# Query maxima of the first six head pairs: from a product with minus the identity to rows laid out through DRAM

## The chip, the cores and the metric

One NeuronCore of a Trainium2 chip runs the whole program. The metric is the device time of one execution in microseconds (us); a version's time is the median of its runs. The core has a matrix engine (PE, with its weight loads shown as PEld), a vector engine (DVE), an activation engine (ACT), a general engine (POOL) and a queue engine (SP) from which every DMA of this kernel is issued. Each engine takes its instructions strictly in the order in which the program holds them.

## The reference

Eight batches of eight heads of 576 tokens go through an attention with exponential features; its output goes through a two-layer network with a squared ReLU.

```python
# q, k, v: (8, 8, 576, 64); w_phi: (64, 128); w_in: (512, 2048); w_out: (2048, 512); all float32
def phi(x):
    proj = einsum('bhsd,df->bhsf', x, w_phi)
    proj = proj - max(abs(proj), axis=-1, keepdims=True)
    return concatenate([exp(proj), exp(-proj)], axis=-1)
q_p, k_p = phi(q), phi(k)
kv  = einsum('bhsf,bhsd->bhfd', k_p, v);  z = sum(k_p, axis=2)
num = einsum('bhsf,bhfd->bhsd', q_p, kv)
den = einsum('bhsf,bhf->bhs', q_p, z)[..., None] + 1e-06
x = (num / den) as (4608 tokens, 512)
out = square(maximum(x @ w_in, 0)) @ w_out
```

What matters here is the subtraction in `phi` for the queries: from all 128 features of a token the largest absolute feature of that token is taken away before the two exponentials.

## The kernel before, in words

**Tiling.** Two heads make a pair, and there are 32 pairs `p`, four to a batch. The query tile `q` of a pair has the 64 dimensions of head 0 on partitions 0 to 63, those of head 1 on partitions 64 to 127, and the 576 tokens along the row. The key tile `k` is alike. The network runs over 18 chunks `c` of 256 tokens, each in 8 steps `f` of 256 hidden columns: `gemm1` (24 fp16 products of 128x256, since inputs and weights are split into a high and a low half) and `gemm2` (12 products of 128x512). A chunk can start when the pairs that hold its tokens have put their output into `ring`; chunk 0 needs pairs 0 to 3. The weights come in as raw 1 MB blocks (`raw0i` to `raw7i`, `raw0o` to `raw7o`) and are split by ACT, DVE and POOL (`prep`).

**Early and late pairs.** Pairs 0 to 5 are the early ones (`EARLY = 6`, function `early`), pairs 6 to 31 the late ones (`visit` and `late`). A late pair finds its query maxima on POOL. An early pair goes through these steps:

- `k_main`, `k_tail`, `keys`: features of the keys, with tokens on partitions, their maxima, differences and exponentials `e` and `et`;
- `kv_main`, `ends`, `flip`: the products of key features with `v` and with ones, and a turn of their sum into `kz`;
- `q_main` and `q_tail`: features of the queries with tokens on partitions, wanted only for the maxima. Three reductions on DVE put them into `qm`: columns 0 to 3 for head 0, 4 to 7 for head 1, 128 tokens to a column, and column 8 for the last 64 tokens of both heads;
- `q_proj`, twice (`c` = 0 and 1, 288 tokens each): the features again, now with features on partitions, in the PSUM tile `pp`. To this product the kernel adds a second one that takes the maxima away: a column of `qm`, broadcast as weights, times `nident`, minus the identity. A column holds 128 tokens, so each half and head takes three of these products (L665);
- `num` and `dens`, with the exponentials `qe` of that tile; the denominators go out of `sx` through DRAM (`den`, `rd`) and come back as rows `rb`; POOL multiplies, and ACT and DVE write `ring`.

**Order.** The code does not fix the order. Every step is an `Op` with an engine, a planned duration, what it comes after, the buffers that it uses and a rank. `Plan.order` lays the steps out on the five engines by these numbers, and `Plan.improve` moves ranks at random 400 times and keeps what shortens its plan. The program is then written in the order of planned starts, so another set of steps or durations gives another order on every engine, for DMAs on SP too. Tiles have few buffers: `pp` is one, `q` and `k` two, `qe` three. In `Plan.add` for a DMA, `land` is the planned time to its landing.

Of the kernel before, what the change touches and what calls it, by code (L numbers as in the profile page):

```python
# [14 lines left out]
F32 = mybir.dt.float32  # L15
# [11 lines left out]
B, H, S, D = 8, 8, 576, 64  # L27
# [12 lines left out]
SH = S // 2  # L40
# [20 lines left out]
WHOLE, ROWS, COLS, STRIPS = range(4)  # L61
# [196 lines left out]
def dve_us(n):  # L258
    return (n + 151) / 960
# [15 lines left out]
def tile_kernel(ctx, tc, qp, kp, vp, w_phi, w_in, w_out, out):  # L275
    nc = tc.nc
    V, A, G, PE, SP = nc.vector, nc.scalar, nc.gpsimd, nc.tensor, nc.sync
    P = Plan()

    cp = ctx.enter_context(tc.tile_pool(name="const", bufs=1))  # L280
    at = ctx.enter_context(tc.tile_pool(name="attn", bufs=1))
    mp = ctx.enter_context(tc.tile_pool(name="moe", bufs=1))
    sm = ctx.enter_context(tc.tile_pool(name="small", bufs=1))
    dr = ctx.enter_context(tc.tile_pool(name="scratch", bufs=1, space=DRAM))
    ps = ctx.enter_context(tc.tile_pool(name="psum", bufs=1, space=PSUM))

    def sub(eng, out_, a, b_):
        eng.tensor_tensor(out=out_, in0=a, in1=b_, op=ALU.subtract)  # L288

    def tiles(pool, tag, shape, dtype, bufs, first=0):  # L290
        return Tiles(P, pool, tag, shape, dtype, bufs, first)

    ident = cp.tile([128, 128], F32, name="ident")
    ones = cp.tile([128, 32], F32, name="ones")
    nident = cp.tile([128, 128], F32, name="nident")
    mask = cp.tile([128, 2, 32], F32, name="mask")
    wraw = cp.tile([128, 3 * F], F32, name="wraw")
    wbf, wst = wraw[:, 0:2 * F], wraw[:, 2 * F:]
# [15 lines left out]
    kmt_ = tiles(sm, "kmt", [128, 1], F32, 2)  # L314
    kvs_ = tiles(at, "kvs", [128, 384], F32, 1)
    kz_ = tiles(at, "kz", [128, 384], F32, 2)
    pt_ = tiles(at, "pt", [128, 2, S], F32, 1, EARLY)
    mx_ = tiles(at, "mx", [128, S], F32, 1, 2 * EARLY)
    qe_ = tiles(at, "qe", [128, 2 * S], F32, 3)
    n_ = tiles(at, "n", [128, S], F32, 1)  # L320
    yt_ = tiles(at, "yt", [128, S], F32, 1, None)
# [9 lines left out]
    den_ = tiles(sm, "den", [128, 9], F32, 2)  # L331
    rc_ = tiles(sm, "rc", [128, 9], F32, 2)
    rd_ = tiles(dr, "rd", [128, 9], F32, 3)
    td_ = tiles(dr, "td", [128, 256], F32, 2, EARLY)
    rb_ = tiles(at, "rb", [128, S], F32, 2)
    vm_ = tiles(sm, "vm", [128, NP], F32, 2)
    pw_ = tiles(sm, "pw", [128, 2], F32, 2)
    qm_ = tiles(sm, "qm", [128, 9], F32, 2)

    pp_ = tiles(ps, "pp", [128, 2, 512], F32, 1, None)  # L340
    pn_ = tiles(ps, "pn", [128, 512], F32, 1, None)
# [9 lines left out]
    dq = cp.tile([32, 2, 32], F32, name="dq")  # L351
    make_identity(nc, ident)
    V.memset(ones, 1.0)
# [144 lines left out]
    exps, exp_t, sums, kz_of, qexp, dens_of, k_load, q_load, num_in = {}, {}, {}, {}, {}, {}, {}, {}, {}  # L500
# [78 lines left out]
    def early(p):  # L579
# [3 lines left out]
        R = lambda x: base + x  # L583
# [21 lines left out]
        o = P.add("PE", 1.73, lambda: kv_main(p, pv_["s", p]), exps[p] + [v_load[p]], kv[:-1], R(2.0), mode=COLS)  # L605
        o = P.add("PE", 1.66, ends, [o, exp_t[p]], kv, R(2.5), mode=(COLS, STRIPS))
# [7 lines left out]
        o = P.add("PE", 0.35, flip, [o, pool_start], [("kvs", p), ("pv", ("t", p))], R(3.0))  # L614
# [5 lines left out]
        most = []  # L620
# [27 lines left out]
        qe = lambda c: qe_[2 * p + c].rearrange("p (h s x) -> p h s x", h=2, s=2)
        for c in range(2):
            n = 2 * p + c  # L650
            cs = slice(SH * c, SH * c + SH)
            pq = ("pp", ("q", n))

            def q_proj(n=n, cs=cs):
                for h in range(2):
                    PE.matmul(out=pp_["q", n][:, h, 0:SH], lhsT=wst[64 * h:64 * h + 64, :],
                              rhs=q_[p][64 * h:64 * h + 64, cs], start=True, stop=False)
                for h in range(2):
                    for t in range(5):
                        lo, hi = max(cs.start, 128 * t), min(cs.stop, 128 * t + 128)  # L660
                        if lo < hi:

                            i, r, d = (4 * h + t, 0, lo - 128 * t) if t < 4 else (8, 64 * h, 64 * h)
                            rows = slice(r, 128 if t < 4 else r + 64)
                            PE.matmul(out=pp_["q", n][:, h, lo - cs.start:hi - cs.start],  # L665
                                      lhsT=qm_[p][rows, i:i + 1].to_broadcast([rows.stop - r, 128]),
                                      rhs=nident[rows, d:d + hi - lo], start=False, stop=hi == cs.stop)
# [4 lines left out]
            o = P.add("ACT", act_us(576), lambda c=c, src=src: A.activation(
                out=qe(c)[:, :, 1, :], in_=src(), func=AF.Exp, scale=-1.0), [o], [("qe", n), pq], R(x + 0.4))
            qexps.append(P.add("ACT", act_us(576), lambda c=c, src=src: A.activation(
                out=qe(c)[:, :, 0, :], in_=src(), func=AF.Exp), [o], [("qe", n), pq], R(x + 0.4)))
# [27 lines left out]
        use = [("sx", ("d", p))]  # L703
# [126 lines left out]
    def late(p):  # L830
# [21 lines left out]
        def q_proj():  # L852
# [4 lines left out]

        o = P.add("PE", 0.98, q_proj, [q_load[p]], [("q", p)] + pq, R(RQ), mode=ROWS)
        pt = [P.add("ACT", act_us(1024), lambda: A.activation(
            out=pt_[p][:, :, 0:512], in_=pp_["Q", p], func=AF.Copy), [o], [pq[0], ("pt", p)], R(RQ + 0.1))]  # L860
        for h in range(2):
            pt.append(P.add("ACT", act_us(64), lambda h=h: A.activation(  # L862
                out=pt_[p][:, h, 512:S], in_=tail(h), func=AF.Copy), [o], [pq[1 + h], ("pt", p)], R(RQ + 0.1)))
        qexp[p], dens = [], []
        for h in range(2):
            n = 2 * p + h
            qe = lambda s, n=n: qe_[n][:, S * s:S * s + S]
            o = P.add("POOL", par_us(S), lambda n=n, h=h: G.partition_all_reduce(  # L868
                mx_[n], pt_[p][:, h, :], channels=128, reduce_op=bass_isa.ReduceOp.absmax),
                [pt[0], pt[1 + h], pool_next], [("pt", p), ("mx", n)], R(RQ + 0.2), lock=0.0)  # L870
            o = P.add("DVE", dve_us(S), lambda n=n, h=h, qe=qe: sub(V, qe(0), pt_[p][:, h, :], mx_[n]),
                      [o], [("pt", p), ("mx", n), ("qe", n)], R(RQ + 0.3), lock=4.0)
# [13 lines left out]
            o = P.add("DVE", dve_us(S), lambda n=n, y=y: V.transpose(yt_["y", n - 2 * EARLY], y()), [o], [("pt", p), ("yt", ("y", n - 2 * EARLY))], R(RQ + 0.9))  # L886
# [170 lines left out]
```

## Time and profile before

| | |
|---|---|
| median of 3 runs | 1089.73 us (1088.62 to 1090.1) |
| the profiled execution | 1087.31 us, of which the span from first to last instruction is 1085.5 us |
| mean granted TensorE clock | 0.997 |
| PE busy | 1063.7 us (98%) |
| DVE, ACT, POOL busy | 737.3, 632.9, 185.6 us |
| first `gemm1` starts at | 100.62 us |

All durations below are of the one profiled execution, which took 2.42 us less than the median. A group's row gives line, engine, operation, output and input tiles, shapes and count. A row of the timeline gives start, duration, engine, line, operation, and in brackets the idle time ahead of it with what ended it. Neighbouring PE rows overlap, because matmuls are pipelined: the time that a step takes is the distance from its start to the next start.

### The profile page before, as it was taken

The page shows a single profiled execution, that of the slowest core. Times are in us where ns is not written, and L with a number is a line of the kernel's source. Part 1 is how long each engine was busy: PE and PEld are TensorE (multiplying, and loading weights), DVE is VectorE, ACT ScalarE, POOL GpSimd, SP SyncE. Part 2 cuts the span into 40 slices and gives each one's busy share as a digit, 9 for nine tenths or more (in the row PEclk, how much of TensorE's full clock was granted, in tenths as well). Part 3 has the DMA queues.
Part 4 walks back from the last instruction along what each step waited for, and adds up shares of the span by engine and source line. Part 5 has one row for each costly group of instructions (what it writes and reads, how often), then busy time and mean ns, then how long its engine had stood idle before and what let it go on. Part 6 is the DMA issues. An engine that isn't in the chain of part 4 may idle for free.

```text
span 1085.5 us, 19971 instructions
## 1 busy us (share of the span) xinstructions
PE 1063.7 (98%) x7882; PEld 826.3 (76%) x7882; DVE 737.3 (68%) x1537; ACT 632.9 (58%) x1125; POOL 185.6 (17%) x87
## 2 busy tenths in 40 slices
PE   7889999999999999999999999999999999999997
PEld 6656777777777777777777777877777777888886
DVE  4589989787778877877878776776777855112111
ACT  6889864466566665656556655665555645333232
POOL 1366531111111111111111111111100111000000
PEclk9999999999999999999999999999999999999999
DMA  8844412212212122222222111112120101000000
GB/s 304 309 126 117 149 46 68 59 35 56 85 45 85 46 75 55 69 62 57 74 56 75 55 60 38 54 55 75 43 63 22 50 14 41 1 21 20 1 20 20
DMA packets 68288, 73.49 MB, mean 68 GB/s; under 512 B 36836, under 2 KB 41828, under 8 KB 68196
## 3 DMA queue, kind: packets, MB, share of 16 engines
q1 hardware_dynamic: 68196, 72.23, 21.8%
q8 instruction: 62, 1.02, 0.4%
q14 instruction: 30, 0.25, 0.1%
HBM read 59.18 MB, written 12.99 MB: 66 GB/s over the span
## 4 chain that ended last, share of the span: by engine, by line
PE 88%; DVE 4%; ACT 3%; DMA 2%; issue 1%; POOL 1%; SPq 0%; DVEq 0%; POOLq 0%
PE po L962 35%; PE ph L934 33%; PE pv L568 4%; PE pp L512 3%; PE pn L786 3%; PE pp L855 3%; PE pv L786 2%; PE pv L573 1%; PE pp L665 1%; PE pn L518 1%; DVE u L415 1%; DMA k<-in_kp_dram 1%; DMA den<-sx 1%; ACT u L412 1%; POOL u L426 1%
## 5 line engine op out<-in xcount | busy, mean ns | idle before, releaser
L934 PE MATMUL ph<-ring,win 128*128 128x256 f16 x3456 | 399.4, 273 | 0.1
L934 PEld LDWEIGHTS <-win 128*128 128x128 f16 x3456 | 328.2, 98 | 67.9 <-issue 30.2
L962 PE MATMUL po<-wout,gh 128*128 128x512 f32 x1152 | 369.6, 402 | 0.0
L962 PEld LDWEIGHTS po<-wout,gh 128*128 128x128 f32 x1152 | 206.8, 189 | 47.8 <-issue 5.6
L943 ACT ACTIVATE r<-ph,cw 128x512 f32<-128x512 f32 x144 | 98.8, 686 | 234.1 <-PE ph L934 233.9
L962 PE MATMUL po<-wout,gl 128*128 128x512 f32 x576 | 226.3, 393 | 0.0
L868 POOL PARTITION_ALL_REDUCE mx<-pt x52 | 113.6, 2184 | 634.3 <-ACT pt L862 528.3
L288 DVE TENSOR_TENSOR gl<-ph,gh 128x512 fp32r<-128x512 f32 x144 | 98.7, 686 | 166.1 <-ACT ph L952 163.5
L962 PEld LDWEIGHTS po<-wout,gl 128*128 128x128 f32 x576 | 108.1, 188 | 25.1 <-DVE gl L288 0.5
L945 ACT ACTIVATE gh<-r 128x512 fp32r<-128x512 f32 x144 | 90.9, 631 | 4.6
L952 ACT ACTIVATE ph<-r 128x512 f32<-128x512 f32 x128 | 74.7, 583 | 0.0
L808 ACT ACTIVATE n<-pn 128x320 f32<-128x320 f32 x26 | 11.4, 438 | 102.4 <-PE pn L786 102.4
L568 PE MATMUL pv<-e,v 128*64 128x256 f32 x512 | 60.9, 380 | 0.4 <-ACT kz L615 0.4
L882 DVE SCALAR_TENSOR_TENSOR pt<-qe,zc,pt 128x576 f32<-128x576 f32 x52 | 42.2, 813 | 22.4 <-ACT pt L880 21.4
L288 DVE TENSOR_TENSOR qe<-pt,mx 128x576 f32<-128x576 f32 x52 | 39.2, 754 | 22.6 <-POOL mx L868 22.3
L534 ACT ACTIVATE e<-e 128x512 f32<-128x512 f32 x64 | 39.8, 621 | 21.4 <-DVE e L531 21.2
L568 PEld LDWEIGHTS pv<-e,v 128*64 128x64 f32 x512 | 35.5, 137 | 15.1 <-ACT kz L615 0.5
L873 ACT ACTIVATE qe<-qe 128x576 f32<-128x576 f32 x52 | 35.0, 673 | 17.2 <-DVE qe L288 17.1
L819 DVE STREAM_TRANSPOSE kvs<-pv 128x256 f32<-128x256 f32 x26 | 11.6, 445 | 47.7 <-PE pv L786 44.4
L880 ACT ACTIVATE pt<-qe,zc 128x576 f32<-128x576 f32 x52 | 39.6, 771 | 3.3
L886 DVE STREAM_TRANSPOSE yt<-pt 128x576 f32<-128x576 f32 x52 | 40.4, 776 | 1.3
L536 ACT ACTIVATE e<-e 128x512 f32<-128x512 f32 x64 | 40.2, 629 | 1.7
(196 smaller groups left out, 1296.0 us busy)
## 6 DMA issues: line engine op xcount, KB each, us to landing
v<-in_vp_dram SPq DMA_DIRECT2D x32, 320.0 KB
k<-in_kp_dram SPq DMA_DIRECT2D x32, 288.0 KB
q<-in_qp_dram SPq DMA_DIRECT2D x32, 288.0 KB
rb<-rd SPq DMA_DIRECT2D x64, 144.0 KB
out_dram<-o SPq DMA_DIRECT2D x36, 256.0 KB
td<-kvs SPq DMA_DIRECT2D x26, 128.0 KB
kz<-td SPq DMA_DIRECT2D x208, 16.0 KB
raw0i<-in_w_in_dram SPq DMA_DIRECT2D x1, 1024.0 KB
```

Source lines behind the costliest of these rows:

```text
L288: eng.tensor_tensor(out=out_, in0=a, in1=b_, op=ALU.subtract)
L536: exps[p].append(P.add("ACT", act_us(512), lambda n=n: A.activation(out=e_[n][:, :, 0, :], in_=e_[n][:, :, 0, :], func=AF.Exp), [o], [("e" ...
L568: PE.matmul(out=to[64 * h:64 * h + 64, 0:256], lhsT=v_[p][:, t, h, :], rhs=e_[2 * p + h][:, t].rearrange("p s f -> p (s f)"), start=t == 0 ...
L786: PE.matmul(out=to[64 * h:64 * h + 64, :], lhsT=kz_[n][:, 128 * s_ + 64 * h:128 * s_ + 64 * h + 64], rhs=qe_[2 * n + h].rearrange("p (s x) ...
L868: o = P.add("POOL", par_us(S), lambda n=n, h=h: G.partition_all_reduce(mx_[n], pt_[p][:, h, :], channels=128, reduce_op=bass_isa.ReduceOp. ...
L882: o = P.add("DVE", dve_us(S), lambda h=h, qe=qe, y=y: V.scalar_tensor_tensor(out=y(), in0=qe(1), scalar=zc_[p][:, 2 * h + 1:2 * h + 2], in ...
L886: o = P.add("DVE", dve_us(S), lambda n=n, y=y: V.transpose(yt_["y", n - 2 * EARLY], y()), [o], [("pt", p), ("yt", ("y", n - 2 * EARLY))], ...
L934: PE.matmul(out=ph[:, j, :], lhsT=win[w][:, t, 128 * ff:128 * ff + 128], rhs=ring[half][x][:, t, c0:c0 + T], start=k == 0, stop=k == 3 * K ...
L943: o = P.add("ACT", act_us(512, 1), lambda: A.activation(out=r_[n], in_=ph_[bank], func=AF.Relu, scale=cw[:, f, 0:1]), [g1], [("ph", bank), ...
L945: sq = P.add("ACT", act_us(512), lambda: A.activation(out=gh_[n], in_=r_[n], func=AF.Square), [o], [("r", n), ("gh", n)], Q)
L952: o = P.add("ACT", act_us(512), lambda: A.activation(out=ph_[bank], in_=r_[n], func=AF.Square), [sq], [("ph", bank), ("r", n)], Q)
L962: PE.matmul(out=po_[po[i][1]], lhsT=g[n][:, j, 128 * i:128 * i + 128], rhs=wout[f][w][:, j, :], start=(ff == 0 and s == 0), stop=(ff == 2 ...
```

## The change

`nident` and the products with it go. After the three reductions DVE turns `qm` (now a tile of 32 columns, two of them, `qm0` and `qm1`, zero beyond column 8) in blocks of 32x32 into `qt`, so that the maxima of 32 tokens stand in one row. SP writes `qt` to a DRAM tile `tq` (first hop). SP then lays the 576 maxima of each head with three DMAs out of `tq` into one row of `pt_[0]`: partition 0 for head 0, partition 64 for head 1; all other rows of that tile are zero (second hop). `q_proj` then needs one more product per head and half: weights of 64 rows of -1 (`minus`, broadcast) times the 64 rows of `pt_[0]`, 288 columns wide (L679). `pt` is otherwise the query tile of the late pairs; its numbers move by one for them, and it is one buffer before and after. The plan gets a planned duration for each of these steps. Memsets for `minus`, `qm0`, `qm1` and `pt_[0]` are added at the start on DVE.

```diff
+QLAND = 2.4
-    nident = cp.tile([128, 128], F32, name="nident")
+    minus = cp.tile([128, 1], F32, name="minus")
+    qm = [cp.tile([128, 32], F32, name=f"qm{i}") for i in range(2)]
...
+    V.memset(minus, -1.0)
+    for x in qm:
+        V.memset(x, 0.0)
+    V.memset(pt_[0], 0.0)
...
-    minus = P.add("DVE", 0.25, lambda: V.tensor_scalar(out=nident, in0=ident, scalar1=-1.0, scalar2=None, op0=ALU.mult),
-                  [pool_start], [], 0.8)
...
-                out=qm_[p][:, 4 * h:4 * h + 4], in_=q_to(h).rearrange("p (t f) -> p t f", t=4),
+                out=qm[p % 2][:, 4 * h:4 * h + 4], in_=q_to(h).rearrange("p (t f) -> p t f", t=4),
...
+        o = P.add("DVE", 0.15, lambda: V.transpose(qt_[p], qm[p % 2]), most, [("qm", p), ("qt", p)], R(1.2))
+        row_of = lambda h, cs: pt_[0][64 * h:64 * h + 64, p % 2, cs]
+        o = P.add("SP", 0.45, lambda: SP.dma_start(tq_[p], qt_[p]), [o], [("qt", p), ("tq", p)], R(1.2), land=QLAND)
+        def spread_rows():
+            for h in range(2):
+                SP.dma_start(pt_[0][64 * h:64 * h + 1, p % 2, 0:512].rearrange("o (t a x) -> o t a x", t=4, a=4),
+                             tq_[p].rearrange("(a c) x -> c a x", a=4)[4 * h:4 * h + 4].unsqueeze(0))
+            SP.dma_start(pt_[0][0:128:64, p % 2, 512:S].rearrange("h (a x) -> h a x", a=2),
+                         tq_[p].rearrange("(h a c) x -> c h a x", h=2, a=2)[8])
+        most = P.add("SP", 1.9, spread_rows, [o], [("tq", p), ("row", p), ("pt", 0)], R(1.2), land=QLAND)
...
                 for h in range(2):
-                    for t in range(5):
-                        lo, hi = max(cs.start, 128 * t), min(cs.stop, 128 * t + 128)
-                        if lo < hi:
-                            i, r, d = (4 * h + t, 0, lo - 128 * t) if t < 4 else (8, 64 * h, 64 * h)
-                            rows = slice(r, 128 if t < 4 else r + 64)
-                            PE.matmul(out=pp_["q", n][:, h, lo - cs.start:hi - cs.start],
-                                      lhsT=qm_[p][rows, i:i + 1].to_broadcast([rows.stop - r, 128]),
-                                      rhs=nident[rows, d:d + hi - lo], start=False, stop=hi == cs.stop)
+                    PE.matmul(out=pp_["q", n][:, h, 0:SH], lhsT=minus[64 * h:64 * h + 64, :].to_broadcast([64, 128]), rhs=row_of(h, cs),
+                              start=False, stop=True)
-            o = P.add("PE", 2.2, q_proj, [q_load[p], minus] + most, [("q", p), pq, ("qm", p)], R(x), mode=(ROWS, WHOLE))
+            o = P.add("PE", 1.1, q_proj, [q_load[p], most], [("q", p), pq, ("row", p), ("pt", 0)], R(x), mode=ROWS)
```

The new steps make another plan, so instructions move on every engine. Line numbers grow by 5 to 13. Three places follow, first before, then after. In the rows of DVE `qm_75` and `qm_76` are `qm0` and `qm1`.

On PE, around a `q_proj` of pair 0 (before its second half, after its first; `kvs` and `m` are the turn of `kv` and two scale steps that stand nearby):

```order
L600 MATMUL pv_222<-et_173,mask 32x128 x4
L656 MATMUL pp_276<-q_118,wraw 128x288 x2
L665 MATMUL pp_276<-nident,qm_171 128x96
L665 MATMUL pp_276<-nident,qm_171 128x128
L665 MATMUL pp_276<-nident,qm_171 128x64
```

At the same place after the change:

```order
L605 MATMUL pv_331<-et_270,mask 32x128 x4
L380 MATMUL pn_383<-ident,m_0_101 128x128
L676 MATMUL pp_390<-q_125,wraw 128x288 x2
L679 MATMUL pp_390<-pt_95,minus 128x288 x2
L617 MATMUL pv_408<-ident,kvs_400 128x128 x3
```

Three products for each head become one, and the first `q_proj` of pair 0 moves from directly behind `k_main` of pair 1 to behind the whole `kv` work of pair 1 (`et_270` is its tail).

On DVE, around the maxima of pair 0 (`km`, `kmt`, `e`, `et` belong to the keys):

```order
L638 TENSOR_REDUCE qm_171<-ph_136 128x4
L642 TENSOR_REDUCE qm_171<-pn_175 128x1
L362 TENSOR_SCALAR nident<-ident 128x128
L528 TENSOR_REDUCE km_206<-po_180 128x4
L531 TENSOR_TENSOR e_210<-po_180,km_206 128x4x128
L528 TENSOR_REDUCE km_216<-po_182 128x4
```

At the same place after the change:

```order
L643 TENSOR_REDUCE qm_75<-ph_143 128x4
L533 TENSOR_REDUCE km_204<-po_179 128x4
L536 TENSOR_TENSOR e_212<-po_179,km_204 128x4x128
L533 TENSOR_REDUCE km_217<-po_181 128x4
L647 TENSOR_REDUCE qm_75<-pn_214 128x1
L652 STREAM_TRANSPOSE qt_235<-qm_75 128x32
L643 TENSOR_REDUCE qm_76<-ph_194 128x4
```

The last reduction of pair 0 now stands behind key work of pair 1, and the turn follows it.

On SP, where the denominators of pair 0 come back (`den_0`, `rd_0`, `rb_0`), with buffer numbers:

```order
L721 DMA rd_0_493<-rc_0_489 128x9
L403 DMA raw7i_495<-in_w_in_dram 128x4x512
L728 DMA rb_0_524<-rd_0_493 64x2x288 x2
L505 DMA q_3_527<-in_qp_dram 128x576
L504 DMA k_5_599<-in_kp_dram 128x576
L469 DMA v_7_615<-in_vp_dram 128x640
L708 DMA den_1_634<-sx_8_631 128x1x9
```

At the same place after the change:

```order
L510 DMA q_3_567<-in_qp_dram 128x576
L734 DMA rd_0_584<-rc_0_564 128x9
L474 DMA v_7_586<-in_vp_dram 128x640
L408 DMA raw7i_591<-in_w_in_dram 128x4x512
L741 DMA rb_0_632<-rd_0_584 64x2x288 x2
L721 DMA den_1_635<-sx_7_615 128x1x9
L655 DMA tq_2_642<-qt_2_593 128x32
L509 DMA k_5_652<-in_kp_dram 128x576
L659 DMA pt_0_95<-tq_2_642 1x16x32 x2
L661 DMA pt_0_95<-tq_2_642 2x2x32
```

The two hops of pair 2 now stand behind the return of pair 0's denominators and behind `den_1`; the load of `q_3` moved ahead of them.

More of the change, by code (lines that the diff above doesn't have):

```diff
@@ L316, in tile_kernel @@
     kz_ = tiles(at, "kz", [128, 384], F32, 2)
-    pt_ = tiles(at, "pt", [128, 2, S], F32, 1, EARLY)
+    pt_ = tiles(at, "pt", [128, 2, S], F32, 1)
     mx_ = tiles(at, "mx", [128, S], F32, 1, 2 * EARLY)
@@ L333, in tile_kernel @@
     rd_ = tiles(dr, "rd", [128, 9], F32, 3)
+    tq_ = tiles(dr, "tq", [128, 32], F32, 2)
     td_ = tiles(dr, "td", [128, 256], F32, 2, EARLY)
@@ L337, in tile_kernel @@
     pw_ = tiles(sm, "pw", [128, 2], F32, 2)
-    qm_ = tiles(sm, "qm", [128, 9], F32, 2)
+    qt_ = tiles(sm, "qt", [128, 32], F32, 2)
+    P.bufs["qm"] = P.bufs["row"] = 2
     pp_ = tiles(ps, "pp", [128, 2, 512], F32, 1, None)
@@ L642, in early @@
         most.append(P.add("DVE", dve_us(128), lambda: V.tensor_reduce(
-            out=qm_[p][:, 8:9], in_=pn_["qt", p][:, 0:128], op=ALU.max, axis=AX.X,
+            out=qm[p % 2][:, 8:9], in_=pn_["qt", p][:, 0:128], op=ALU.max, axis=AX.X,
             apply_absolute_value=True), [o], [("pn", ("qt", p)), ("qm", p)], R(1.1)))
+        o = P.add("DVE", 0.15, lambda: V.transpose(qt_[p], qm[p % 2]), most, [("qm", p), ("qt", p)], R(1.2))
[8 more added lines that the diff above has]
+        most = P.add("SP", 1.9, spread_rows, [o], [("tq", p), ("row", p), ("pt", 0)], R(1.2), land=QLAND)
         nums, qexps = [], []
@@ L859, in late @@
         pt = [P.add("ACT", act_us(1024), lambda: A.activation(
-            out=pt_[p][:, :, 0:512], in_=pp_["Q", p], func=AF.Copy), [o], [pq[0], ("pt", p)], R(RQ + 0.1))]
+            out=pt_[p - EARLY + 1][:, :, 0:512], in_=pp_["Q", p], func=AF.Copy), [o], [pq[0], ("pt", p - EARLY + 1)], R(RQ + 0.1))]
         for h in range(2):
             pt.append(P.add("ACT", act_us(64), lambda h=h: A.activation(
-                out=pt_[p][:, h, 512:S], in_=tail(h), func=AF.Copy), [o], [pq[1 + h], ("pt", p)], R(RQ + 0.1)))
+                out=pt_[p - EARLY + 1][:, h, 512:S], in_=tail(h), func=AF.Copy), [o], [pq[1 + h], ("pt", p - EARLY + 1)], R(RQ + 0.1)))
         qexp[p], dens = [], []
@@ L868, in late @@
             o = P.add("POOL", par_us(S), lambda n=n, h=h: G.partition_all_reduce(
[L869 to L872, printed above, removed]
+                mx_[n], pt_[p - EARLY + 1][:, h, :], channels=128, reduce_op=bass_isa.ReduceOp.absmax),
+                [pt[0], pt[1 + h], pool_next], [("pt", p - EARLY + 1), ("mx", n)], R(RQ + 0.2), lock=0.0)
+            o = P.add("DVE", dve_us(S), lambda n=n, h=h, qe=qe: sub(V, qe(0), pt_[p - EARLY + 1][:, h, :], mx_[n]),
+                      [o], [("pt", p - EARLY + 1), ("mx", n), ("qe", n)], R(RQ + 0.3), lock=4.0)
             o = P.add("ACT", act_us(S), lambda qe=qe: A.activation(out=qe(1), in_=qe(0), func=AF.Exp, scale=-1.0),
@@ L877, in late @@
             qexp[p].append(o)
-            use = [("qe", n), ("zc", p), ("pt", p)]
-            y = lambda h=h: pt_[p][:, h, :]
+            use = [("qe", n), ("zc", p), ("pt", p - EARLY + 1)]
+            y = lambda h=h: pt_[p - EARLY + 1][:, h, :]
             o = P.add("ACT", act_us(S, 1), lambda h=h, qe=qe, y=y: A.activation(
@@ L884, in late @@
                 op0=ALU.mult, op1=ALU.add), [o], use, R(RQ + 0.8), lock=4.0)
-            o = P.add("DVE", dve_us(S), lambda n=n, y=y: V.transpose(yt_["y", n - 2 * EARLY], y()), [o], [("pt", p), ("yt", ("y", n - 2 * EARLY))], R(RQ + 0.9))
+            o = P.add("DVE", dve_us(S), lambda n=n, y=y: V.transpose(yt_["y", n - 2 * EARLY], y()), [o], [("pt", p - EARLY + 1), ("yt", ("y", n - 2 * EARLY))], R(RQ + 0.9))
             dens.append(P.add("DVE", dve_us(S), lambda n=n, h=h: V.tensor_reduce(
```

## The prediction

> **What bounds the kernel now.** I read the table of stretches first, then PE's timeline up to the first chunk of the network, and last the chain of waits and SP's timeline for the price of a hop.
>
> ```profile
> 0.00:100.60 100.60, 85.32 (x883) 59.00 (x883) 69.57 (x123) 82.63 (x141) 41.62 (x23) 0.98 0.67 228
> 100.60:160.00 59.40, 58.46 (x470) 44.45 (x469) 53.59 (x89) 46.13 (x74) 30.42 (x12) 1.00 0.30 94
> 160.00:1035.00 875.00, 874.93 (x6244) 685.84 (x6242) 605.51 (x1315) 489.67 (x889) 113.58 (x52) 1.00 0.18 50
> 1035.00:1085.50 50.50, 44.95 (x292) 37.03 (x290) 8.68 (x12) 14.47 (x24) 0.00 (x0) 0.97 0.06 21
> ```
>
> After the length, the columns of a stretch are the busy time of PE, PEld, DVE, ACT and POOL, then granted clock, DMA share and GB/s. Length less busy time, PE idles for 21.8 us in all. From 100.6 to 1035 us it idles for only 1.0 us: there the end is PE's work, and nothing else can be gained or lost. The last stretch holds 5.5 us of idle at the tail, which the change does not touch. The other 15.3 us lie before 100.6, where the change acts. In that stretch ACT is busy for 82.63 us, nearly as long as PE, so PE's lead there is thin. The end of that stretch is this, on DVE
>
> ```profile
> 98.27 1.74 DVE L758 SCALAR_TENSOR_TENSOR ring<-rb,cb,ring 128x576 f16<-128x576 f32 x1
> ```
>
> and on PE, in the timeline:
>
> ```profile
> 100.62 2.79 PE L934 MATMUL ph<-ring,win 128*128 128x256 f16 x24
> ```
>
> The last write of pair 3 to `ring` lets the first `gemm1` start at 100.62. From then on PE always has network work to fall back on. So the time is the start of that first `gemm1`, plus PE's work that is still left then, plus what it idles later.
>
> **What PE saves.** These are PE's rows for one stretch at full clock; the start-to-start distances are my price list (`q_main` has the shape of `k_main`, L512).
>
> ```profile
> 25.34 1.06 PE L512 MATMUL po<-wraw,k 64*128 64x128 f32 x16
> 26.33 1.19 PE L682 MATMUL pn<-qe,kz 128*64 128x288 f32 x8
> 27.35 1.90 PE L568 MATMUL pv<-e,v 128*64 128x256 f32 x16
> 29.08 0.39 PE L633 MATMUL pn<-wraw,q 128*64 128x128 f32 x4
> 29.30 0.60 PE L573 MATMUL pv<-et,v 128*64 128x256 f32 x4
> 29.83 1.08 PE L600 MATMUL pv<-e,ones 128*32 128x128 f32 x32
> 30.73 0.40 PE L600 MATMUL pv<-et,mask 128*32 128x128 f32 x8
> 30.94 1.15 PE L700 MATMUL pn<-qe,kz 128*32 128x288 f32 x16
> 32.03 0.75 PE L656 MATMUL pp<-q,wraw 64*128 64x288 f32 x4
> 32.71 1.52 PE L665 MATMUL pp<-nident,qm 128*128 128x128 f32 x12
> 34.07 0.53 PE L612 MATMUL pv<-ident,kvs 128*128 128x128 f32 x3
> 34.53 0.44 PE L518 MATMUL pn<-wraw,k 128*64 128x128 f32 x4
> ...
> 36.30 0.76 PE L656 MATMUL pp<-q,wraw 64*128 64x288 f32 x4 [0.24 <-ACT qe L674]
> 36.99 2.07 PE L665 MATMUL pp<-nident,qm 128*128 128x96 f32 x12
> 38.99 1.19 PE L682 MATMUL pv<-qe,kz 128*64 128x288 f32 x8
> ```
>
> The products with minus the identity take 1.36 us in the first half (32.71 to 34.07) and 2.00 us in the second (36.99 to 38.99). The new product has the shape of L656: 64 rows, 288 columns, both heads on their own halves of the rows, 0.69 us (36.30 to 36.99). A pair saves 1.36 + 2.00 - 2 x 0.69 = 1.98 us, and six pairs 11.9 us. The sums by line bound this from above: all L665 products are busy for 23.13 us, all L656 products, which the new ones copy, for 10.06, a difference of 13.1. These are the sum rows of two tables of stretches over the first 160 us, of L665 and of L656:
>
> ```profile
> sum 160.00, PE 23.13 PEld 19.80; mean PE 5.78 PEld 4.95
> ```
>
> ```profile
> sum 160.00, PE 10.06 PEld 4.07; mean PE 2.52 PEld 1.02
> ```
>
> What lies between 11.9 and 13.1 is mainly the slow first pair, on a PE that has only just begun; another step will stand in its place and be slow, so I take 11.9. Were the two heads not to overlap, a half would take up to twice 0.69 and a pair would save only 3.36 - 2.76 = 0.6 us; the L656 rows, on the same halves of the array, speak against that.
>
> **What DVE pays.** Six turns of 128x32 are added and one scaling of the identity goes. No row shows that turn. Its bounds are a memset of 128x32 and a turn of 128x256:
>
> ```profile
> 0.80 0.09 DVE L353 MEMSET ones<- 128x32 f32 x1 [0.80 <-PEq L1047]
> ```
>
> ```profile
> 150.26 0.44 DVE L819 STREAM_TRANSPOSE kvs<-pv 128x256 f32<-128x256 f32 x1
> ```
>
> I take 0.2, since a turn of an eighth of the width is nearer to the short end. Three of the six fall behind 50 us, where DVE is nearly full: 0.6 us on the path (0.3 to 1.3).
>
> The memset of `pt_[0]`, 1152 columns, costs at most 36 x 0.09 = 3.2 us and lies where DVE waits for the first keys: nothing. Were that cover gone, `km` would start later by the excess.
>
> ```profile
> 6.66 0.69 DVE L528 TENSOR_REDUCE km<-po 128x4 f32<-128x512 f32 x1 [5.36 <-PE po L512]
> ```
>
> **What the two hops cost.** A pair now issues one DMA out to DRAM and three back, and SP waits for the first to land before it issues the other three. Behind that wait stand the loads of keys, values and raw weights, and the return of denominators.
>
> ```profile
> 33.26 6.96 DMA den<-sx
> 40.70 4.22 DMA rd<-rc
> 45.67 3.60 DMA rb<-rd
> ```
>
> ```profile
> 54.98 0.32 SPq L721 DMA_DIRECT2D rd<-rc  x1
> 55.40 0.38 SPq L505 DMA_DIRECT2D q<-in_qp_dram  x1
> 56.40 1.26 SPq L728 DMA_DIRECT2D rb<-rd  x2
> ```
>
> The first three rows are the denominators of pair 0, sent while raw weights fill the queues: 3.6 to 7.0 us a hop. The last three are pair 1, on emptier queues: `rd` is issued at 54.98, and by 56.40 its reader goes out, 1.42 us for a hop. An issue of `rb` takes 0.63, so three take 1.9. Both hops cost 2 x 1.42 + 1.9 = 4.7 us at the light price and up to 7.0 + 4.2 + 1.9 = 13.1 at the loaded one.
>
> Skill and row differ here. The Trainium skill, page "DMA: Bandwidth & Descriptors", section "Anatomy of one DMA — SWDGE (gpsimd) path", gives a DMA of that path a fixed part of about 2.0 us, most of it the receipt of the write, longest into HBM, which speaks against two hops through DRAM. By that estimate a pair pays 5.9 us in place of 4.7, and the stall below grows by 1.2; the 1.42 us of `rd`, a write into DRAM sent from SP, is below the page's figure, and the sum goes by it.
>
> Whether PE waits depends on what the order lays between the turn and `q_proj`. For pair 0 the maxima are ready where PE ends `q_tail`, near 15 us (PE starts at 4.57, k and q of two pairs on a slow clock and `kv_main` follow). Between the turn and the first `q_proj` PE then has `kv_main`, the tail and ones, `flip`, `k_main`, `kv_main`, tail and ones again: 1.73 + 0.53 + 1.11 + 0.46 + 0.99 + 1.73 + 0.53 + 1.11 = 8.2 us, and it waits about 2 us there for exponentials of pair 1. Rows at 15.5 + 8 (between the two prices, since 1 MB blocks are under way) land at about 24, PE asks at 26: no stall. The rows of pair 1 are asked for some 9 us later, and its hops follow directly: none.
>
> Pair 2 is the tight one. Its turn comes near 43, but on SP it stands behind `rd_0`, `rb_0` and `den_1`. In the row above `rb` went out at 45.67, and I let it slip no more, so the first hop of pair 2 goes out at about 46.5 and the rows land at 46.5 + 4.7 = 51.2. By the price list PE's work up to there (five `k_main`, four each of `q_main`, `kv_main` and halves of `q_proj`, two each of `num` and `dens`, and the small ones, 36 us, 3 of slow start, 4 of idle after 4.57) ends at 47.7. Stall: 3.5 us; its bounds are 0 and 46.5 + 13.1 - 47.7 = 11.9. Pairs 3 to 5 meet light queues, with more than 4.7 us of other PE work behind their turns: none. The tile `pt`, now shared with the late pairs, is free in time: PE's first late `q_proj` stands three `gemm1` behind the last early one. SP's 24 added issues cost 15 us of an engine that does nothing else.
>
> **The sum.** -11.9 (PE) + 3.5 (pair 2) + 0.6 (DVE) = -7.8 us. The profiled execution would come to 1087.31 - 7.8 = 1079.5, the median to 1089.73 - 7.8 = 1081.9. As a check: before its first `gemm1` PE had 85.3 us of work; five pairs save 9.9, and in the new order `kv_main`, tail, ones and `flip` of pair 5 (3.8 us) come ahead of it: 79.2 left. With 15.3 of idle and the stall of 3.5 the first `gemm1` starts at 98.0, 2.6 earlier, and 3.8 + 2.0 less is left after it (pair 5): 8.4, or 7.8 with DVE's 0.6.
>
> **Rivals.**
>
> *ACT sets the start of the network.* ACT's 82.63 us up to 100.6 stay, and the new order puts about five more of its steps (some 3 us at 0.6 each) ahead of the first `gemm1`. If ACT's 18 us of idle do not shrink, that `gemm1` stays at 100.6 or so. What is left then is the 3.8 us of pair 5 brought forward and its own 2.0 saved: -5.8, 1083.9. For it speaks how close ACT is to PE; against it the chain of waits of the last 20 us ahead of that `gemm1`, where the line of the old products leads and the first of ACT comes far behind:
>
> ```profile
> by line: PE pp L665 16.5%; PE pn L682 11.1%; DVE u L415 7.0%; PE pp L656 6.5%; PE pv L600 5.8%; DVE km L528 5.7%; PE pv L682 5.7%; PE pp L512 5.3%; PE pn L700 5.3%; PE pv L568 5.1%; ACT win L448 5.0%; ACT qe L672 3.1%; ACT e L536 3.0%; DVE
> ```
>
> *The clock drops in the stall.* After a wait of 1.81 us PE ran slower:
>
> ```profile
> 66.00:76.00 10.00, 8.06 (x55) 5.40 (x53) 9.57 (x13) 9.18 (x16) 7.09 (x3) 0.83 0.35 111
> ```
>
> ```profile
> 71.28 1.86 PE L682 MATMUL pn<-qe,kz 128*64 128x288 f32 x8 [1.81 <-DVE et L541]
> 73.06 1.33 PE L656 MATMUL pp<-q,wraw 64*128 64x288 f32 x4
> 74.33 2.41 PE L665 MATMUL pp<-nident,qm 128*128 128x96 f32 x12
> ```
>
> The `num` took 0.67 more than the 1.19 above, the L656 group 0.57 more than 0.76, the L665 group 0.34 more than 2.07: about 1.6 us lost. A stall of 3.5 would do the same: -6.2, 1083.5. The Trainium skill, page "TensorE: Matmul & The Clock Gate", section "HAM oscillation — how this bites in real kernels", has the rule: gaps above some 3.4 us make PE run at half clock until it has been busy again. Here a wait of half that length was enough.
>
> *No change.* PE's saved time turns into idle before and after the first `gemm1`, as DVE (53.59 of 59.4 us there) and ACT keep their pace: 1089.7.
>
> *Slower: SP's queue.* The first hop of pair 2 holds SP at the loaded price, and `k_5`, `rd_1` and the next raw block wait behind it: 11.9 us of stall, 1.6 of clock, 0.6 on DVE and 2.6 at pair 0 (rows at 15.5 + 13.1 = 28.6 against 26) come to 16.7 against the saved 11.9: +4.8, 1094.5. It decides once PE stalls for more than 11.9 - 0.6 + 2.2 = 13.5 us in all; for it speaks that the loaded rows stand in this trace, against it that a hop was down to 1.42 us by 56 us.
>
> **How the numbers follow.** A measurement of this kernel can tell about 0.2%, 2.2 us. My forecast has 0.48, ACT 0.17, the clock 0.08, no change 0.12, slower 0.15. So faster has 0.73, same 0.12, slower 0.15. The range starts at 1076: with no stall and the full 13.1 saved, less 0.6, the median comes to 1077.2, and its three runs lie up to 1.1 us below it. It ends at 1091.5, past no change, and leaves out most of the slower case.
>
> **What would show it.** The L679 group at about 0.69 us a half; the first `gemm1` near 98 us or earlier; the rows of `pt` about 4.7 us behind the hop out; a wait of PE before the `q_proj` of pair 2 and none at the other pairs; the stretch after the first `gemm1` with no more than 1 us of idle. I am wrong if PE waits for rows at several pairs, if the first `gemm1` stays beyond 100 us, or if PE idles after it.

## Result and profile after

The prediction was 1081.9 us, faster. The changed kernel takes 1094.55 us (median of 6 runs, 1093.01 to 1097.05) against 1088.49 us for the kernel before on the same chip: a ratio of 1.0063, 95% interval 1.0043 to 1.0083. It is slower, and it lies beyond the upper end of the range, 1091.5.

The stretches of the changed kernel, cut at its first `gemm1` as those of before were:

```profile
0.00:109.49 109.49, 81.60 (x867) 51.30 (x868) 76.69 (x132) 86.81 (x146) 42.04 (x24) 0.92 0.65 213
109.49:160.00 50.51, 47.30 (x358) 36.13 (x356) 44.89 (x80) 35.57 (x56) 25.38 (x11) 1.00 0.27 82
160.00:1035.00 875.00, 873.01 (x6228) 683.34 (x6227) 611.64 (x1323) 495.13 (x897) 114.80 (x54) 1.00 0.18 52
1035.00:1092.60 57.60, 52.17 (x340) 42.71 (x338) 9.94 (x14) 16.28 (x27) 0.00 (x0) 0.98 0.05 19
```

PE is busy for 1054.1 us in all, 9.6 less than before, and idle for 38.5 instead of 21.8. The idle that matters is again ahead of the first `gemm1`: 27.9 us instead of 15.3. Its mean clock there is 0.92 instead of 0.98. Behind it, up to 1035 us, PE idles for 5.2 us where it idled for 1.0. A first `gemm1` beyond 100 us and idle after it are two of the three signs by which the prediction said that it would be wrong. The first `gemm1`, on PE's timeline of the changed kernel, comes almost 9 us later than before and then stops for one of DVE's writes:

```profile
109.49 1.26 PE L947 MATMUL ph<-ring,win 128*128 128x256 f16 x10
111.92 1.69 PE L947 MATMUL ph<-ring,win 128*128 128x256 f16 x14 [1.17 <-DVE ring L771]
```

What was built does what it says. On PE's timeline one half of a `q_proj` is

```profile
30.66 0.76 PE L676 MATMUL pp<-q,wraw 64*128 64x288 f32 x4
31.24 0.65 PE L679 MATMUL pp<-pt,minus 64*128 64x288 f32 x4
31.82 1.19 PE L695 MATMUL pn<-qe,kz 128*64 128x288 f32 x8
```

so the new products take 0.58 us a half (31.24 to 31.82). On SP's timeline, the hops of pair 2:

```profile
50.90 0.42 SPq L655 DMA_DIRECT2D tq<-qt  x1
...
53.85 1.37 SPq L659 DMA_DIRECT2D pt<-tq  x2
55.26 0.54 SPq L661 DMA_DIRECT2D pt<-tq  x1
```

PE wants those rows at 62.82 (below) and does not wait. In the whole trace PE waits for rows at no pair. These are the longest waits of PE up to 130 us; the third column is the sum, then the count and the longest:

```profile
PE pn L380 <- ACT raw2i L449: 7.2, 1, 7.2
PE po L517 <- DMA k<-in_kp_dram: 6.8, 2, 4.3
PE pn L380 <- DVE qm L647: 2.6, 1, 2.6
PE pv L573 <- ACT e L541: 2.1, 2, 1.4
PE pn L713 <- DVE qm L647: 1.8, 1, 1.8
```

The longest is new. On PE's timeline it stands in front of a scale product (L380, `power`):

```profile
49.73 0.44 PE L523 MATMUL pn<-wraw,k 128*64 128x128 f32 x4
57.37 0.79 PE L380 MATMUL pn<-ident,wm 128*128 128x128 f32 x2 [7.21 <-ACT raw2i L449]
58.10 3.68 PE L573 MATMUL pv<-e,v 128*64 128x256 f32 x16
61.71 1.28 PE L676 MATMUL pp<-q,wraw 64*128 64x288 f32 x4
62.82 0.65 PE L679 MATMUL pp<-pt,minus 64*128 64x288 f32 x4
```

and on ACT's timeline its cause:

```profile
46.47 0.41 ACT L719 ACTIVATE sx<-pn 128x288 f32<-128x288 f32 x1 [1.29 <-PE pn L713]
46.86 0.49 ACT L620 ACTIVATE kz<-pv 128x384 f32<-128x384 f32 x1
53.23 0.74 ACT L480 ACTIVATE sx<-v 128x640 bf16<-128x640 f32 x1 [5.89 <-DMA den<-sx]
```

`sx` is one tile with two users: ACT copies the denominators of a pair into it (L719) for the DMA `den`, and the size step of `v` (L480) uses it as scratch. ACT stood still for 5.89 us until `den_1` had read it. The chain of waits of the changed kernel from 37 to 58 us says why `den_1` was late:

```profile
37.07 5.97 DMA den<-sx
...
43.06 1.07 DVE den L730
...
44.39 4.38 DMA rd<-rc
...
48.79 0.69 SPq L741
...
50.22 2.94 DMA den<-sx
...
53.23 0.83 ACT sx L480 x2
...
56.28 1.05 ACT raw2i L449 x2
57.33 0.04 issue
57.37 0.79 PE pn L380 x2
```

On SP it stood behind `rb_0` (L741), which waited for the round trip of pair 0's denominators, 5.97 and 4.38 us a DMA while raw weights were loading. No hop of the change stands in this chain. It is the new order, as the fifth experiment shows without the hops: PE's `dens` of pair 1 and ACT's L719 came earlier, and the size step was put right behind.

### The profile page after: what moved, and what is told of

It reads as the page before. It is cut to its first block, busy times and chain, and to the rows that moved or that the text cites. A ratio compares the mean times of both kernels' runs of the same rounds, so it can differ in the third digit from the quotient of the medians.

```text
span 1092.6 us, 19825 instructions
## 1 busy us (share of the span) xinstructions
PE 1054.1 (96%) x7786; PEld 813.5 (74%) x7786; DVE 743.2 (68%) x1546; ACT 633.8 (58%) x1125; POOL 182.2 (17%) x87
## 4 chain that ended last, share of the span: by engine, by line
PE 85%; DVE 6%; DMA 4%; ACT 3%; issue 1%; POOL 0%; SPq 0%; DVEq 0%; ACTq 0%
PE po L975 35%; PE ph L947 32%; PE pv L573 4%; PE pn L799 3%; PE pp L868 2%; PE pp L517 2%; PE pv L799 2%; DVE u L420 1%; DMA den<-sx 1%; PE pv L578 1%; PE pn L523 1%; DMA k<-in_kp_dram 1%; DVE u L424 1%; DMA raw7o<-in_w_out_dram 1%; ACT e L541 0%
## 5 line engine op out<-in xcount | busy, mean ns | idle before, releaser
L821 ACT ACTIVATE n<-pn 128x320 f32<-128x320 f32 x26 | 11.4, 437 | 97.1 <-PE pn L799 97.1
L573 PE MATMUL pv<-e,v 128*64 128x256 f32 x512 | 63.9, 388 | 2.1 <-ACT e L541 2.1
```

The costliest lines, as they stand in the source:

```text
L573: PE.matmul(out=to[64 * h:64 * h + 64, 0:256], lhsT=v_[p][:, t, h, :], rhs=e_[2 * p + h][:, t].rearrange("p s f -> p (s f)"), start=t == 0 ...
```

## Experiments

Ratios are to the kernel before on the same chip. First, the scratch: the order is kept, and only the tile changes.

```diff
-   out=sx_["va", p]...
+   out=(yt_ if p < 8 else sx_)["va", p]...
```

> The changed kernel, its order on every engine kept; only the scratch output of ACT's size step of v (whose values nobody reads) goes for pairs 0 to 7 to another tile than the one from which the denominators leave by DMA. Theory A (the loss is PE's 7.2 us wait at 50 us: ACT held until the DMA of pair 1's denominators has left the shared tile): the wait and part of the clock drop behind it go, the first gemm1 starts near 104 in place of 111.9, the time falls by 5 to 9 us to 1086 to 1090. Theory B (the new order asks too much of ACT and DVE everywhere, this wait is only where it shows first): another wait takes its place, less than 2 us are won. Theory C (the hops hold SP): no change, 1093 to 1096.

1090.4 us, 1.0023 (1.0009 to 1.0038). The size step now runs at once on ACT, and PE's wait is half as long, for DVE:

```profile
48.96 0.73 ACT L480 ACTIVATE yt<-v 128x640 bf16<-128x640 f32 x1
```

```profile
55.10 0.77 PE L380 MATMUL pn<-ident,wm 128*128 128x128 f32 x2 [3.40 <-DVE et L546]
```

The scratch is worth 0.4%, some 4 us of the 6, a little less than theory A had. The first `gemm1` starts at 106.14 us, not at 104, and `kv_main` behind the shorter wait still takes 3.57 us.

Second, no wait for the landings of the first hops: the rows come from an input that is there from the start. SP still waits for the turns.

```diff
-   ... tq_[p].rearrange(...)
+   ... kp[p][:, 0:32].rearrange(...)
```

> The changed kernel, its order kept; the first hop is still written, but the rows are read from 128 rows of 128 bytes of the key input in place of it, so SP never waits for the first hop's landing, and PE's rows do not depend on the maxima (the maxima are thus not taken away). Theory C (SP's waits for the six first hops, 16.0 us in all, push back the loads and the denominators behind them): the time falls by 5 us or more, to 1089 or below, and the first denominators leave SP earlier than 37.07. Theory A: the denominators of pair 0 still meet the raw blocks, less than 3 us are won, 1092 to 1096.

1093.26 us, 1.0054 (1.0035 to 1.0073), with 7.1 us of the same wait at L380. SP's waits for these landings cost about 1 us, less than these runs can tell from nothing. SP's waits for the turns (L655) are still there, 8.6 us in all.

Third, only the short products, in the order of before and without turn or hops:

```diff
-   for t in range(5): ... PE.matmul(lhsT=qm_[p][rows, i:i + 1]..., rhs=nident[...])
+   PE.matmul(out=pp_["q", n][:, h, 0:SH], lhsT=qm_[p][64 * h:64 * h + 64, 8:9].to_broadcast([64, 128]),
+             rhs=wraw[64 * h:64 * h + 64, 0:SH], start=False, stop=True)
```

> The kernel before, its order kept; only its products with minus the identity are replaced by one product per head and half of the new shape (64 rows, 288 columns), with the last column of the maxima as weights and the projection weights as data, so no turn, no hops, and wrong maxima. It measures what the shorter products are worth alone. If PE bounds the first 100 us, as the prediction had it: 11.9 us less, about 1076.5. If ACT and DVE pace it: the first gemm1 stays within 3 us of 100.6 and the time between 1084 and 1088.

1087.62 us, 0.9998 (0.9982 to 1.0013). Here PE's saving, with nothing paid for it, buys nothing that these runs can tell. These are the sum rows of the first 130 us, of the kernel before and of this one:

```profile
sum 130.00, PE 114.24 PEld 81.96 DVE 96.96 ACT 109.95 POOL 61.43; mean PE 114.24 PEld 81.96 DVE 96.96 ACT 109.95 POOL 61.43
```

```profile
sum 130.00, PE 105.44 PEld 70.79 DVE 97.70 ACT 110.61 POOL 62.47; mean PE 105.44 PEld 70.79 DVE 97.70 ACT 110.61 POOL 62.47
```

PE has 8.8 us less to do by 130 us and idles for 8.8 us more; DVE and ACT are only 0.7 us ahead. The first `gemm1` starts at 99.23 us instead of 100.62, and PE's clock ahead of 100.6 us is 0.93 instead of 0.98. The chain of waits of this kernel from 30 to 101 us is made mostly of denominators' DMAs, DVE, ACT and POOL:

```profile
by line: DMA den<-sx 9.1%; DMA rd<-rc 6.4%; DVE u L415 5.2%; DMA rb<-rd 5.0%; issue 5.0%; PE pn L675 4.8%; POOL u L426 4.8%; PE pv L675 4.7%; POOL rb L729 4.6%; ACT u L412 4.4%; ACT win L448 2.9%; PE pv L568 2.4%; ACT qe L665 2.2%; ACT ring
```

Fourth, only turn and hops, in the order of before, issued right behind the last reduction and read by nobody (with the wider `qm` and the shared `pt` that they need):

```diff
+   V.transpose(yt_["qt", p][:, 0:32], qm[p % 2])
+   SP.dma_start(tq_[p], yt_["qt", p][:, 0:32])
+   SP.dma_start(pt_[0][...], tq_[p]...)   # three of them
```

> The kernel before, its order kept, old products kept; the turn and the four DMAs of the two hops are added directly behind the last reduction of each early pair, and nobody reads the rows. It measures what the hops cost by holding SP and filling the queues. Theory C: slower than before by 3 us or more, since SP stands for up to 13 us at pairs 0 and 1 in front of the raw blocks. Theory A or B: within 2 us of before, since SP's queue has slack.

1121.04 us, 1.03 (1.0271 to 1.0329). Each hop waits at the head of SP's queue for a turn and a landing that lie ahead of it; SP's longest waits up to 130 us:

```profile
SPq L654 <- DVE yt L653: 17.2, 4, 7.0
SPq L656 <- DMA tq<-yt: 14.3, 5, 6.1
```

The changed kernel's same two waits are:

```profile
SPq L659 <- DMA tq<-qt: 16.0, 6, 6.6
SPq L655 <- DVE qt L652: 8.8, 4, 5.6
```

The landings cost SP as much there, the waits for the turn half, and the second experiment found no measurable loss by the landings. So hops cost three per cent here, in a queue whose order was made without them. The whole change in the order of before was not tried.

Fifth, the order by itself: the changed kernel's order with the work of before in it. The steps of turn and hops stay in the plan and issue nothing.

```diff
-   lambda: V.transpose(qt_[p], qm[p % 2])   and both SP steps
+   lambda: None                            # nident is made at the first of them
-   PE.matmul(... minus ..., rhs=row_of(h, cs) ...)
+   for t in range(5): ...                  # the products of before
```

> The order of the changed kernel with the work of the kernel before: the ten short subtracting products, no turn, no hop, no rows (values unchanged). Theory O (the new order of the work alone carries the 6 us): 1.0045 to 1.0085, the wait of 7 us at the power product stays, the first gemm1 at 108 to 111 us. Theory H (what the change itself issues, the hops on SP's queue above all, carries it): 0.998 to 1.002, first gemm1 near 101. Between the two, 1.002 to 1.0045: each has a share.

1098.25 us, 1.0095 (1.0069 to 1.0122). The order alone costs more than the whole change does. The wait behind the scratch is there too, and it ends almost where it ended in the changed kernel, since PE does not set its end:

```profile
51.15 0.44 PE L522 MATMUL pn<-wraw,k 128*64 128x128 f32 x4
57.98 0.80 PE L379 MATMUL pn<-ident,wm 128*128 128x128 f32 x2 [6.39 <-ACT raw2i L448]
```

PE reached it 1.4 us later (51.15 against 49.73) and left it 0.6 us later: more than half of the time saved by then was waited away at this one place.

The planner searches orders by random trials; another start of them (`SEED`) gives another order for the same work.

```diff
-TRIALS, SEED, MOVED = 400, 1, 70.0
+TRIALS, SEED, MOVED = 400, 2, 70.0      # 3, 4
```

> The changed kernel whole, with another start of the planner's random trials (2 instead of 1), so another order. Theory O (one unlucky order): a draw of its own, anywhere in 0.995 to 1.012, and the 7 us wait at the power product behind the shared scratch need not be there. Theory H (the change's own work costs): again 1.004 to 1.009.

> The kernel before with the same other start of the trials. Theory O: as far from 1.000 as the changed kernel's draws are from each other, 0.996 to 1.010; this says how much an order alone moves the time of one and the same work. Theory H: 0.999 to 1.002, the order matters little.

> The changed kernel whole, with a third start of the planner's trials. Theory O (the time is that of the order drawn, the change itself is worth 0.1 to 0.4 per cent at one order): 1.000 to 1.009, and 0.996 to 1.000 of the kernel before with the same start. Theory H (the change's own work costs, whatever the order): 1.004 to 1.009 and above the kernel before with the same start.

> The kernel before with the third start. Theory O: 1.001 to 1.012, the order on which the kernel before runs is a good one among its draws, and above the changed kernel with the same start by 0.1 to 0.4 per cent. Theory H: 0.999 to 1.002.

> The kernel before with a fourth start of the planner's trials. Theory O (before's own order is one of its good draws): 1.003 to 1.015. Rival (starts 2 and 3 were the odd ones): 0.998 to 1.002.

> The changed kernel whole with a fourth start of the planner's trials. Theory O: a draw, 0.998 to 1.009, and 0.1 to 0.8 per cent under the kernel before with the same start. Theory H (the change's own work costs): above the kernel before with the same start.

| start | kernel before | changed kernel |
|---|---|---|
| 1 | 1 | 1.0063 (1.0043 to 1.0083) |
| 2 | 1.0062 (1.0039 to 1.0085) | 1.0051 (1.0026 to 1.0075) |
| 3 | 1.0146 (1.0104 to 1.0189) | 1.0070 (1.0046 to 1.0093) |
| 4 | 1.0038 (1.0025 to 1.0052) | 1.0096 (1.0076 to 1.0117) |

The order that the kernel before runs in is the best of its four; the other three are slower by 0.4 to 1.5% with the same work. The changed kernel is faster at start 3 and slower at starts 1 and 4; at start 2 the two can't be told apart. The spread was larger than expected: 1.0146 and 1.0096 lie above the ranges given for them. "0.1 to 0.8 per cent under the kernel before with the same start" failed at the fourth: two plans of one start share no order, so they are two draws. The longest wait of PE ahead of the network differs with the order too: in the changed kernel 7.2, 4.6, 8.6 and 7.9 us at the four starts, each for an ACT or DVE result.

To compare at one and the same order, the work of before was put into the changed kernel's orders of starts 2 and 3 too, and into the first order with the scratch apart.

> Before's work (ten short products, no turn, no hop) in the order that the changed kernel has with start 2, where the changed kernel itself took 1.0051. Theory S (at one order the change saves 0.2 to 0.5 per cent): 1.007 to 1.010. Theory N (it saves nothing, the difference of 0.3 per cent at the first order was chance): 1.003 to 1.007.

> Before's work in the order that the changed kernel has with start 3, where the changed kernel itself took 1.0070. Theory S: 1.009 to 1.012. Theory N: 1.005 to 1.009.

> Before's work in the changed kernel's order, with the scratch of v's size step apart for pairs 0 to 7; with the scratch shared this took 1.0095. Theory A (the scratch that holds ACT is about 4 us of the order's price): 1.004 to 1.007, and no wait of PE over 5 us on ACT's raw copies. Rival (the 4 us were won only together with the short products): 1.008 to 1.010.

| order | work of before | work of the change | PE busy | PE idle |
|---|---|---|---|---|
| start 1 | 1.0095 (1.0069 to 1.0122) | 1.0063 (1.0043 to 1.0083) | 1067.2, 1054.1 | 27.1, 38.5 |
| start 2 | 1.0083 (1.0061 to 1.0104) | 1.0051 (1.0026 to 1.0075) | 1069.9, 1056.3 | 25.8, 34.8 |
| start 3 | 1.0089 (1.0072 to 1.0106) | 1.0070 (1.0046 to 1.0093) | 1069.3, 1056.5 | 27.2, 36.2 |
| start 1, scratch apart | 1.0052 (1.0032 to 1.0073) | 1.0023 (1.0009 to 1.0038) | 1067.1, 1057.0 | 24.0, 30.8 |

The last two columns are us of the profiled executions, work of before first. At one order the change saves 0.32, 0.32, 0.19 and 0.29%. No single pair settles that, as the intervals of the first three overlap, and 1.0089 at start 3 lies in the range that was expected if the change saves nothing. All four together give 0.28%, or 0.13 to 0.43% if their errors are independent, which they are not wholly, as some pairs share runs of the kernel before: some 3 us. PE is relieved by 10.1 to 13.6 us, and 6.8 to 11.4 us of it come back as idle. These pairs price the change's work whole, turn and hops with it. The short products without the hops were not run in a new order, so how much of the lost relief the hops take there is open. The sum rows of the first 130 us show the same in time order, for the work of before in the new order and for the changed kernel:

```profile
sum 130.00, PE 109.91 PEld 76.17 DVE 93.00 ACT 103.19 POOL 53.50; mean PE 109.91 PEld 76.17 DVE 93.00 ACT 103.19 POOL 53.50
```

```profile
sum 130.00, PE 99.91 PEld 66.21 DVE 96.58 ACT 104.15 POOL 55.60; mean PE 99.91 PEld 66.21 DVE 96.58 ACT 104.15 POOL 55.60
```

By 130 us the relieved PE has idled 10.0 us more. ACT has done 1 us and DVE 3.6 us more, so they are a little ahead, not ten. The chains of waits from 20 us to the first `gemm1` change hands accordingly: with the work of before the old products lead,

```profile
by line: PE pp L678 14.3%; PE pv L572 7.8%; issue 7.0%; PE pp L669 6.3%; PE pv L604 5.3%; DMA rd<-rc 4.7%; PE pn L695 3.7%; PE pn L713 3.5%; ACT u L416 3.4%; DMA den<-sx 3.3%; DVE ring L771 3.2%; PE pv L695 2.4%; DVE u L423 2.3%; PE pv L577
```

and in the changed kernel the denominators' DMA and DVE:

```profile
by line: DMA den<-sx 15.1%; DVE u L420 11.1%; issue 10.3%; DMA v<-in_vp_dram 5.0%; DMA rd<-rc 4.9%; PE pv L573 4.0%; DVE u L424 3.9%; ACT e L541 3.8%; DVE ring L771 3.8%; PE pn L713 3.6%; ACT e L539 3.0%; ACT sx L480 2.6%; ACT win L453 2.3%
```

Last come four attempts at something better: the scratch apart with the planner told of it (at starts 1 and 2), and the planner's landing times moved toward the traced ones, for both kernels.

```diff
-   ("sx", ("va", p))
+   ("yt" if p < 8 else "sx", ("va", p))
...
-QLAND = 2.4;  den land=2.2;  rd land=2.2;  rb land=3.5
+QLAND = 3.4;  den land=3.8;  rd land=3.5;  rb land=4.5     # the last two runs only
```

> The changed kernel with the scratch of v's size step apart for pairs 0 to 7 (in yt), and the planner told of it, so that it orders anew. Theory A (the shared scratch that held ACT is the largest single piece): 0.998 to 1.002, no wait of over 4 us on ACT's raw copies before the first gemm1. Theory B (the new order asks too much of ACT and DVE wherever the scratch lies): 1.002 to 1.005, first gemm1 at 104 or later.

> The changed kernel with the scratch apart, the planner told of it, and start 2: an attempt at a version under both kernels. Theory O: a draw, 0.997 to 1.007; under 1.000 it beats both. If the scratch is worth as much here as at start 1 (0.3 to 0.4 per cent under the changed kernel with the same start): 1.001 to 1.002.

> The changed kernel with v's scratch apart (pairs 0 to 7) and with the planner's landing times nearer to what the trace showed of the first 100 us: denominators out 3.8 instead of 2.2 us, their inverses 3.5 instead of 2.2, the spread of them 4.5 instead of 3.5, the new hops 3.4 instead of 2.4. Theory L (the draws are bad because the planner takes landings for shorter than they are, so that SP and ACT wait in order behind them): 0.994 to 1.000. Theory O alone (any new order is a draw, mean near 1.005): 1.001 to 1.009.

> The kernel before with the same scratch and the same three landing times of denominators (no hops). Theory L: 0.994 to 1.000. Theory O alone: 1.001 to 1.010.

The first two took 1090.93 us, 1.0035 (1.0013 to 1.0057), and 1093.95 us, 1.0071 (1.0047 to 1.0094). The scratch is worth 0.4% in a fixed order; at start 2 with a new order nothing is left of it. The landing times gave 1107.18 us, 1.0172 (1.0138 to 1.0207), for the changed kernel and 1099.65 us, 1.011 (1.0078 to 1.0142), for the kernel before: longer landings in the plan do not make better orders, and that theory fell. No version beat the kernel before.

## Why the prediction was wrong

- **The step that failed is the sum.** It was to give -7.8 us and gave about +6.8 (0.63%), for two reasons: a new order was put at nothing and costs 10.3 us (next point), and the change's work at one order is worth about 3.5 us, not 7.8. For the latter, the sum took PE's 11.9 us off the time whole, "with 15.3 of idle" ahead of the first `gemm1` kept as it was. The saving itself was sized well: 0.58 us a half against the 0.69 forecast, and 13.1 us of busy time at the same order, against a bound of 13.1. But the idle time is not a constant. It is what is left between PE and a chain of denominators, ACT and DVE that keeps its own pace, as the short products alone show. Measured, the 11.9 are worth some 3 us in the new orders, and in before's order nothing (0.9998, products alone). My rivals "ACT sets the start" and "no change" had this mechanism, with 0.29 between them.
- **A term was missing, and it is the larger miss: the price of another order.** Every order I showed was read for the hops alone. The order alone costs 0.95%, or 10.3 us of 1087.2, and then the change gives about 3.5 back (0.95 - 0.63 = 0.32%). Of the 10.3 the shared scratch is some 4.7 (1.0095 against 1.0052). Where the other 5.6 lie stays open; many small waits and PE's clock are candidates.
- **The stall of pair 2 (3.5 us) did not come.** The hop went out at 50.90, later than the 46.5 forecast, behind the same `rb_0` and `den_1`. But PE asked at 62.82 instead of 47.7, and 7.2 us of that delay came from the scratch. With the scratch apart it asked at 59.89 us, and did not wait for the rows either.
- **The price of a hop** was right at both ends: 1.42 us at pair 3, 2.95 at pair 2 (above) and up to 6.6 of waiting at others. The 2.0 us that the prediction quotes from the Trainium skill, page "DMA: Bandwidth & Descriptors", section "Anatomy of one DMA — SWDGE (gpsimd) path", are stated for DMAs issued from gpsimd. These go out from SP, and the first was below them, on SP's timeline of the changed kernel:

```profile
69.53 0.33 SPq L655 DMA_DIRECT2D tq<-qt  x1
...
70.95 1.42 SPq L659 DMA_DIRECT2D pt<-tq  x2
```

- **DVE** was right: the turn takes 0.21 us against 0.2, and the memset of `pt_[0]` 1.02 us, under the bound of 3.2 and hidden:

```profile
1.17 1.02 DVE L361 MEMSET pt<- 128x1152 f32 x1 [0.19 <-issue]
...
45.14 0.21 DVE L652 STREAM_TRANSPOSE qt<-qm 128x32 f32<-128x32 f32 x1
```

- **The clock** fell as that rival says, at another wait. After the 7.2 us, `kv_main` (58.10 above) took 3.68 us instead of before's 1.90, and the granted clock was 0.50 from 57.4 to 62.4 us. That agrees with the rule of the Trainium skill, page "TensorE: Matmul & The Clock Gate", section "HAM oscillation — how this bites in real kernels", that the prediction quotes: half clock behind gaps above some 3.4 us.
- **The slower rival gave 1094.5, and its number is right for a wrong reason.** It wanted PE to stall for the rows, and PE never did; taking the waits for the first hops' landings away gave back about 1 us of 6, not told from nothing. SP's queue did matter, through `rb_0` ahead of `den_1`.
- **The range** ended at 1091.5, under that rival. With four starts, an order is worth from 0 to +1.5%; such a spread should have widened the range on the slow side and brought the chance of faster near a half.

## What to carry over

If a change makes a planner lay out all work anew, price the new order as a draw of its own: here draws of one kernel lay 1.5% apart, five times what the change was worth. Measure the parts apart, old work in the new order and new work in a fixed order. And before a saving on the busiest engine is subtracted, ask what its neighbours' chain does with the earlier start: a wait that ends at the same time swallows it.

## What the hardware showed

DVE's long operations beside POOL's were slower than I had allowed for. On DVE's timeline of the changed kernel one and the same operation takes 1.22 us and, two rows on, over 3.3:

```profile
98.67 1.22 DVE L424 SCALAR_TENSOR_TENSOR u<-raw3o,u 128x1024 int32<-128x1024 int32 x1
...
100.53 3.33 DVE L424 SCALAR_TENSOR_TENSOR u<-raw5i,u 128x1024 int32<-128x1024 int32 x1
...
105.70 3.32 DVE L424 SCALAR_TENSOR_TENSOR u<-raw4o,u 128x1024 int32<-128x1024 int32 x1
```

POOL's timeline there:

```profile
100.02 2.75 POOL L431 TENSOR_TENSOR u<-u,raw3o 128x1024 int32<-128x1024 int32 x1 [8.45 <-ACT u L417]
...
105.08 2.86 POOL L431 TENSOR_TENSOR u<-u,raw5i 128x1024 int32<-128x1024 int32 x1
```

POOL's end at 102.77 and 107.94, and DVE's slow ones 1.1 us later each, at 103.86 and 109.02: that is as if DVE ran its own 1.2 us once that POOL instruction was done. The Trainium skill, page "SBUF — State Buffer", section "Terms", has the port pair that both share as an exclusive lock, held for a whole instruction; the rows agree. The write to `ring` that the second part of the first `gemm1` waited for came behind this row of operations.

PE's clock also drops for waits shorter than the 3.4 us of the Trainium skill's rule cited above: with the work of before in the new order and the scratch apart, a wait of 2.90 us was followed by a `kv_main` of 3.16 us instead of 1.90, with a granted clock of 0.64 from 55.6 to 60.3 us:

```profile
55.70 0.49 PE L379 MATMUL pn<-ident,wm 128*128 128x128 f32 x2 [2.90 <-ACT raw2i L448]
56.12 3.16 PE L572 MATMUL pv<-e,v 128*64 128x256 f32 x16
```
